# Residual added by accumulating DMAs, and no planned gap behind the output projection, in a fused attention and feed-forward kernel

## The chip, the cores and the metric

The kernel runs on one core of one Trainium2 chip. The metric is the device time of one execution in microseconds (us), as the median of several runs. The core has TensorE (PE in the profile; its weight loads are PEld), VectorE (DVE), ScalarE (ACT), GpSimd (POOL) and SyncE (SP). SyncE, ScalarE and GpSimd each issue DMAs from a queue of their own; here almost all are issued by SyncE and GpSimd.

## The reference

```python
# x: 1 x 2048 x 640, float32; 32 heads of 20; window of 8 keys, 2 positions apart
xn = layernorm(x)
q, k, v = split(xn @ wqkv)                      # 640 x 1920
logits = q . k[pos - 2 * (0..7)] * 20 ** -0.5   # masked where pos - 2w < 0
o = softmax(logits) . v[pos - 2 * (0..7)]
s = o @ wo                                      # 640 x 640
g = silu(silu(xn @ w1) @ w2)                    # 640 x 1536, 1536 x 640
return x + s * g
```

The last line is the one that matters: a product `s * g` and then the residual `x`.

## The kernel before

The 2048 rows are worked in four groups (0 to 3) of 512 rows, as tiles of 4 x 128 rows. Row tiles are chosen so that a position's window lies in its own partition and its neighbours. All matrix products run in three passes on operands split in a high and a low part (`hi x hi`, `lo x hi`, `hi x lo`), so each weight has two halves. A weight is split on chip at first use (ScalarE makes the high part, VectorE or GpSimd the low part, from a raw copy); its halves are stored to DRAM and loaded from there later (L584, on GpSimd's queue) into a ring of seven slots, `w`. Units of weights are loaded in the order in which TensorE uses them. w1 and w2 are split and stored in the first group; wo is split in the second and third group and loaded in the fourth.

For each group g there are two stages. In the projection stage TensorE makes q, k and v for four quarters of the heads (L1000 to L1002) while VectorE works on the attention: long multiplies and reductions over `pr` (L794, L797, L836, L842). In the feed-forward stage TensorE runs "ups" (w1, L1188 to L1190, into `rot`) and "downs" (w2, L1045 and L1047, into `acc`), with, between up 0 and up 1, the output projection of the group before, `wo_phase(g - 1)`, which also uses L1045 and L1047. After each up, ScalarE writes `sh` and `sf` (L1201, L1202) and VectorE the low part `sl = sf - sh` (L1203), which the last passes of the down read. So the output projection of group 0 lies in the feed-forward stage of group 1 (the second group) and that of group 1 in the stage of group 2 (the third). Those are the two that the change touches; groups 2 and 3 leave by other code (`wo_rest`, `wo_last`).

At the end of `wo_phase` VectorE multiplies the products in PSUM by the gate `G` (named `gate` in the profile), in place (L1084): four of 384 columns and two of 2 x 256. A planner entry named "hold" of HOLD = 3.4 us on VectorE follows; it emits no instruction. Then for each of the four row tiles SyncE loads x into one of three `xr` tiles (L1101), GpSimd adds the gated tile (L1102), and SyncE stores the sum to the output (L1104).

`G` has a second use: its 2560 columns, cut in five pieces of 512, are buffers for the transposes of the next group's normalized x by DMA (ScalarE rearranges, L677; SyncE transposes, L682; ScalarE joins, L690; L696 and VectorE's L697 split into `th` and `tl`). A piece can be taken once the tiles of `G` under it are no longer needed: piece 3 lies under tiles 2 and 3, piece 4 under tile 3. The `xr` tiles also receive raw copies of weights (L548).

The order of each engine's instructions is made ahead of time by a planner, `Weave`: every step is entered with its engine, an estimated duration, a priority, what it reads and writes, and extra times (`late` delays a reader on another engine, `more` is added to a DMA's landing). The planner simulates them in time and then changes the order where its simulated TensorE has a gap. An entry marked `lock` excludes other such entries on VectorE and GpSimd at the same time. The resulting order is fixed on each engine; on the chip an instruction waits, in that order, for what it reads and writes.

Of the kernel before, what the change touches and what calls it, by code (L numbers as in the profile page):

```python
# [15 lines left out]
P = 128  # L16
# [17 lines left out]
XQ = 1  # L34
ADD_LATE = 3
WARM, WARM2 = 20, 3
HOLD = 3.4
LO = 10
FIRST = """00 01 000 001 010 020 011 10 002 012 003 11 013 110 120 014 102 104 111 103 121 021 004 123 20 113 023 21 101 220 114
200 223 202 024 211 204 221 201 124 112 212 100 30 210 203 213 022 122 222 31 214 224 300 301 302 303 304 310 311 312  # L40
# [17 lines left out]
O_OUT = (), (35.0, 55.0), (35.0, 55.0), (10.0, 25.0, 40.0)  # L58
O_BACK = (), (80.0, 82.0), (80.0, 82.0), (40.0, 55.0, 60.0)
O_HOME = {2: {0: -9.0, 1: -6.0, 2: -3.0}}  # L60
BY_SCALAR = True
MULT = 400
WHOLE_O = (2,)
# [9 lines left out]
STORE_Q = 1, 3  # L73
STORE_W2 = ()
RAW_AGAIN = {}
AGAIN_AHEAD = 6
SHARED = (1, 0), (1, 2), (2, 0), (2, 2), (3, 0)
X_AT = 1.2, 6, 8
TILE_AT = 1, 1.5, 5, 6
# [254 lines left out]
def local_attention_silu_ffn(ctx: ExitStack, tc: tile.TileContext, x, wqkv, wo, w1, w2, out):  # L334
# [26 lines left out]
    def tiles(name, n, shape, dtype=F32):  # L361
        return [sb.tile(shape, dtype, name=f"{name}{i}") for i in range(n)]
# [27 lines left out]
    L = tiles("l", 2, [P, T, W, HQ])  # L390
    XIN = sb.tile([P, T, D], F32, name="xin")
    G = sb.tile([P, T, D], F32, name="gate")
    XR = tiles("xr", 3, [P, D])
    SF = sb.tile([P, TOK], F32, name="sf")
    MARK = small("mark", 1)
    TURN = sb.tile([P, TOK], F32, name="turn")
# [26 lines left out]
    def dve(n, fn, reads, writes, prio, lock=False, late=0.0, spans=()):  # L423
        return add("DVE", dv(n), fn, reads, writes, prio, lock, late=late, spans=spans)

    def act(n, fn, reads, writes, prio, table=None, more=0.0, late=0.0, at=0.0, spans=()):
        return add("ACT", ac(n) + more, fn, reads, writes, prio, table=table, late=late, at=at, spans=spans)
# [9 lines left out]
    def dma(fn, reads, writes, nbytes, prio, dur=0.45, more=0.0, quick=0.0, at=0.0):  # L437
        add("SP", dur, fn, reads, writes, prio, nbytes=nbytes, more=more, quick=quick, at=at)
# [71 lines left out]
    def raw_tile(k):  # L510


        if k < DC:
            return "pr", k
        if k < early:
            s = (k - DC) % 6
            return ("xr", s) if s < 2 else ("g", s - 2)
        return "xr", k % 3

    def raw_ap(u, r):  # L520
# [9 lines left out]
    def raw_load(k):  # L530
        i = fresh[k]
        u = units[i]
        n = width(i)
        of, s = raw_tile(k)
        raw_in[of, s] = k
        if of == "pr":
            r, kr = PRV[:, s * n:(s + 1) * n], [PRK[s]]
        elif of == "g":
            r, kr = G[:, s, :n], [("g", s, 0), ("g", s, CA)]
        else:  # L540
            r, kr = XR[s][:, :n], [("xr", s)]
        raws[i] = r, kr
        pairs = [raw_ap(u, r)]
        by = nc.scalar if k in BY_ACT else nc.sync

        def go():
            for to, frm in pairs:
                by.dma_start(to, frm)  # L548
        if k in BY_ACT:
            add("ACT", 0.65 * len(pairs), go, [], kr, -1, nbytes=n * P * 4)  # L550
            return
        dma(go, [], kr, n * P * 4, 1 + k if k < 2 * DC else clock[0] + 5, (0.62 if k < 2 * DC else 0.45) * len(pairs))

    def ahead(i):
        return AGAIN_AHEAD if units[i][0] == "w2" and i > fresh[early] else RAW_AHEAD
# [502 lines left out]
    def gate(ts, cs):  # L1058
        return of(G[:, ts.start] if ts.stop - ts.start == 1 else G[:, ts], cs)

    def gkeys(ts, cs):
        return [("g", t, cs.start) for t in range(ts.start, ts.stop)]
# [3 lines left out]
    def wo_phase(g, i):  # L1066
        banks = tm_banks()
        a, b = banks
        for c in range(DC):
            wh, wl, kh, kl = w_next("wo", c)  # L1070
            for t in range(T):
                def one(c=c, t=t, wh=wh, wl=wl):
                    tm_mm(banks, t, OH[i][:, c, tsl(t)], wh, c == 0, False)
                    tm_mm(banks, t, OH[i][:, c, tsl(t)], wl, False, False)
                    tm_mm(banks, t, OL[i][:, c, tsl(t)], wh, False, c == DC - 1)
                pe(3 * TM, one, t_keys(i, [c], [t]) + [kh, kl], [a[t][1], b[t // 2][1]])
            w_done()
        for p, kp, ts, cs in tm_views(banks):
            n = (ts.stop - ts.start) * (cs.stop - cs.start)
            if g == NG - 2 and BY_SCALAR:  # L1080
                at = of(XIN[:, ts.start] if ts.stop - ts.start == 1 else XIN[:, ts], cs)
                act(n, lambda p=p, at=at: nc.scalar.activation(at, p, AF.Copy), [kp], [("xin", t) for t in range(ts.start, ts.stop)], 0)
                continue
            dve(n, lambda p=p, ts=ts, cs=cs: nc.vector.tensor_tensor(  # L1084
                out=gate(ts, cs), in0=p, in1=gate(ts, cs), op=OP.mult), [kp], gkeys(ts, cs), 0, late=ADD_LATE)
        for t in range(T) if g == NG - 2 and BY_SCALAR else ():
            one = slice(t, t + 1)
            dve(D, lambda t=t: nc.vector.tensor_tensor(out=G[:, t], in0=XIN[:, t], in1=G[:, t], op=OP.mult),
                [("xin", t)], gkeys(one, slice(0, CA)) + gkeys(one, slice(CA, D)), MULT, lock=True)
        if g == NG - 2:  # L1090
            for t in range(T):
                xr, kx = (XR[t], [("xr", t)]) if t < 3 else (PRV[:, :D], PRK)
                rest.append((t, xr, kx))
                if t < 3:
                    dma(lambda t=t, xr=xr: nc.sync.dma_start(xr, rows(xg, g)[:, t, :]), [], kx, P * D * 4, clock[0] + 5, at=clock[0])
            return
        add("DVE", HOLD, lambda: None, [("g", t, CA) for t in range(T)], ["hold"], 0)
        for t in range(T):
            s = take("xr", 3)
            xr = XR[s]  # L1100
            dma(lambda t=t, xr=xr: nc.sync.dma_start(xr, rows(xg, g)[:, t, :]), [], [("xr", s)], P * D * 4, clock[0] + 5)  # L1101
            add("POOL", po(D), lambda t=t, xr=xr: nc.gpsimd.tensor_tensor(out=xr, in0=xr, in1=G[:, t, :], op=OP.add),  # L1102
                [("g", t, 0), ("g", t, CA)], [("xr", s)], 500, lock=True)
            dma(lambda t=t, xr=xr: nc.sync.dma_start(rows(og, g)[:, t, :], xr), [("xr", s)], [], P * D * 4, clock[0] + 20, quick=OUT_IN)  # L1104
# [124 lines left out]
    def ffn_phase(g, i, ix, io):  # L1229
        if g + 1 < NG:  # L1230
            behind = [("kv", XQ, 0)] if g else []
            step = 1 if g in X_SINGLE else 2
            for t in range(0, T, step):
                load_x(g + 1, t, step, behind=behind)
            for t in range(T):
                ln_stats(t)
            ln_rstd(0, T)
            for t in range(T):
                ln_apply(t)
        ps = None  # L1240
        begun = clock[0]
        by_dma = X_DMA.get(g, ())
        bufs = [("buf", c, h) for c in range(DC) for h in range(2)] if g else []
        if not g:
            for k, c in enumerate(by_dma):
                turn_first(c, ix, begun + X0_OUT + X0_PACE * k, begun + X0_BACK + X0_PACE * k)
        for kind, f in plan(g):
            if kind == "w1":
                up(g, i, f, io)
            elif kind == "wo":  # L1250
                wo_phase(g - 1, io)
                if g == NG - 1:
                    turn_os(g, io, begun)
                if g == NG - 1:
                    free_for([("xin", t) for t in range(T)], [("xin", t, c) for t in range(T) for c in (0, CA)])
                for c in range(DC) if by_dma else ():
                    ts = slice(c * TOK // D, ((c + 1) * TOK - 1) // D + 1)
                    free_for(gkeys(ts, slice(0, CA)) + gkeys(ts, slice(CA, D)), bufs[2 * c:2 * c + 2])
                for k, c in enumerate(by_dma):
                    by = (piece(G, X_BY[c]), ("buf", X_BY[c])) if c in X_BY else (TURN, ("turn",))  # L1260
                    turn_x(c, ix, by, (piece(G, c), ("buf", c)), clock[0] + PACE0[g] + PACE * k, clock[0] + BACK[g])
            elif kind == "x":
                if f not in by_dma:
                    split_t(XIN, [("xin", t) for t in range(T)], f, ix, (TH, TL), XIN[:, :, tsl(f)])
            elif kind == "o":
                if f not in O_DMA.get(g, ()):
                    o_chunk(g, f, io)
            elif kind == "rest":
                o_rest(g, f, io)
            else:  # L1270
                ps = ps or tm_banks()
                down(f, ps)
        for p, kp, ts, cs in tm_views(ps):
            n = (ts.stop - ts.start) * (cs.stop - cs.start)
            act(n, lambda p=p, ts=ts, cs=cs: nc.scalar.activation(gate(ts, cs), p, AF.Silu), [kp], gkeys(ts, cs) + bufs * bool(by_dma), 0, "silu")
        if g < NG - 1:
            turn_os(g, i, begun)
            turn_home(g, i)
# [40 lines left out]
```

## Time and profile before

| | |
|---|---|
| median of 3 runs | 597.69 us (597.64 to 597.71) |
| profiled execution, its own time | 598.14 us |
| its span, first to last instruction | 596.0 us |
| PE, PEld busy | 589.7 us (99%), 555.0 us (93%) |
| DVE, ACT, POOL busy | 514.1 (86%), 258.8 (43%), 163.2 us (27%) |
| granted TensorE clock | 1.000 |
| DMA | 165.00 MB, mean 277 GB/s |
| L1102, the residual adds on POOL | 8 of 1560 ns |

A row of a group of instructions gives line, engine, operation, output <- inputs, shape and count, then the busy time in us and the mean ns of one, then the engine's idle time just before them and what ended it. A timeline row gives the start, the duration, the engine, the line and what it writes and reads; "xN" at its end means that N instructions in a row are merged. Matmuls are pipelined, so their durations overlap; the distance between two starts is what one of them costs.

### The profile page before, as it was taken

The numbers are of one execution on the slowest core, as the hardware profiler recorded it, in microseconds if no ns is written. First come the engines' busy times: TensorE is split into PE (matmuls) and PEld (weight loads), VectorE is DVE, ScalarE is ACT, GpSimd is POOL, SyncE is SP. The second block draws the span as 40 slices with busy tenths as digits, with TensorE's granted clock in tenths as the row PEclk, the third lists the DMA queues.
The fourth block names the chain that finished last, engine by engine and source line by source line (L and its number), as shares of the span: only waits on it lengthen the run. The fifth ranks groups of instructions, "written<-read, shape, count | busy, mean of one in ns | idle before, by whom it ended". The sixth has DMA issues, their size and how long they took to land.

```text
span 596.0 us, 9084 instructions
## 1 busy us (share of the span) xinstructions
PE 589.7 (99%) x3431; PEld 555.0 (93%) x3431; DVE 514.1 (86%) x503; ACT 258.8 (43%) x458; POOL 163.2 (27%) x229
## 2 busy tenths in 40 slices
PE   8999999999999999999999999999999999999997
PEld 7999999999999999999999999989999999999997
DVE  6599999999799978999988997999847799999544
ACT  5447465362545323747523605433742254434230
POOL 5800102132210154342321126443122233531100
PEclk9999999999999999999999999999999999999999
DMA  9999999779999999997699999967779999989952
GB/s 287 317 307 333 322 411 394 287 254 292 278 321 315 318 216 231 375 223 217 196 308 310 303 348 308 301 196 232 197 214 291 286 289 261 263 221 316 253 195 89
DMA packets 83527, 165.00 MB, mean 277 GB/s; under 512 B 23213, under 2 KB 47501, under 8 KB 83485
## 3 DMA queue, kind: packets, MB, share of 16 engines
q1 hardware_dynamic: 63645, 84.72, 49.6%
q0 software_dynamic: 19296, 79.31, 45.3%
q8 instruction: 27, 0.44, 0.3%
q10 hardware_dynamic: 544, 0.41, 0.2%
q14 instruction: 15, 0.12, 0.1%
HBM read 107.91 MB, written 34.16 MB: 238 GB/s over the span
## 4 chain that ended last, share of the span: by engine, by line
PE 79%; issue 7%; DMA 7%; DVE 4%; POOL 2%; ACT 0%; SPq 0%; POOLq 0%; DVEq 0%
PE acc L1045 18%; PE acc L1047 12%; PE rot L1188 8%; PE rot L1190 8%; PE rot L1189 8%; PE acc L1000 7%; PE acc L1001 7%; PE acc L1002 7%; DMA half_wo<-w 3%; PE acc L950 2%; DMA w<-half_q 2%; DMA w<-half_w 1%; POOL w L584 1%; DVE pr L794 1%; DVE l L797 1%
## 5 line engine op out<-in xcount | busy, mean ns | idle before, releaser
L1000 PE MATMUL acc<-w,th 128*128 128x480 f32 x300 | 110.4, 368 | 0.0
L1001 PE MATMUL acc<-w,tl 128*128 128x480 f32 x300 | 109.8, 366 | 0.0
L1002 PE MATMUL acc<-w,th 128*128 128x480 f32 x300 | 109.8, 366 | 0.0
L1045 PE MATMUL acc<-w,sh 128*128 128x384 f32 x384 | 108.6, 328 | 0.0
L1047 PE MATMUL acc<-w,sh 128*128 128x256 f32 x384 | 104.7, 273 | 0.0
L794 DVE TENSOR_TENSOR pr<-q,kv 128x2560 f32<-128x2560 f32 x32 | 92.0, 2874 | 10.7 <-DMA kv<-kv 7.9
L836 DVE TENSOR_TENSOR pr<-q,kv 128x2560 f32<-128x2560 f32 x32 | 91.5, 2859 | 1.0
L1188 PE MATMUL rot<-th,w 128*128 128x512 f32 x240 | 91.8, 383 | 0.0
L1189 PE MATMUL rot<-tl,w 128*128 128x512 f32 x240 | 91.0, 379 | 0.0
L1190 PE MATMUL rot<-th,w 128*128 128x512 f32 x240 | 91.0, 379 | 0.0
L797 DVE TENSOR_REDUCE l<-pr 128x128 f32<-128x2560 f32 x32 | 89.7, 2804 | 0.3
L1201 ACT ACTIVATE sh<-rot 128x512 fp32r<-128x512 f32 x48 | 28.8, 599 | 122.2 <-PE rot L1190 122.2
L584 POOL DMA_DIRECT2D w<-half_w x72 | 38.9, 541 | 142.9 <-PE acc L1047 57.2
L1047 PEld LDWEIGHTS acc<-w,sh 128*128 128x128 f32 x384 | 73.7, 192 | 0.6
L1045 PEld LDWEIGHTS acc<-w,sh 128*128 128x128 f32 x384 | 72.6, 189 | 0.6
L1002 PEld LDWEIGHTS acc<-w,th 128*128 128x128 f32 x300 | 56.7, 189 | 4.0
L584 POOL DMA_DIRECT2D w<-half_q x52 | 27.9, 537 | 118.9 <-PE acc L1002 73.5
L1001 PEld LDWEIGHTS acc<-w,tl 128*128 128x128 f32 x300 | 56.7, 189 | 3.9
L1000 PEld LDWEIGHTS acc<-w,th 128*128 128x128 f32 x300 | 56.7, 189 | 3.9
L1045 PE MATMUL acc<-w,sl 128*128 128x384 f32 x192 | 56.0, 329 | 0.0
L1203 DVE TENSOR_TENSOR sl<-sf,sh 128x512 fp32r<-128x512 f32 x48 | 38.7, 807 | 19.0 <-ACT sf L1202 19.0
L1047 PE MATMUL acc<-w,sl 128*128 128x256 f32 x192 | 52.3, 273 | 0.0
(117 smaller groups left out, 1072.8 us busy)
## 6 DMA issues: line engine op xcount, KB each, us to landing
w<-half_w POOLq DMA_DIRECT2D x72, 640.0 KB, 6.8
w<-half_q POOLq DMA_DIRECT2D x52, 480.0 KB, 4.7
half_w<-w SPq DMA_DIRECT2D x24, 640.0 KB
half_q<-w SPq DMA_DIRECT2D x20, 480.0 KB
kv<-kv SPq DMA_DIRECT2D x15, 560.0 KB
w<-half_wo POOLq DMA_DIRECT2D x10, 640.0 KB, 8.3
kv<-kv SPq DMA_DIRECT2D x15, 420.0 KB
gate<-in_B_w_dram SPq DMA_DIRECT2D x16, 320.0 KB
```

The source lines that it names most:

```text
L584: add("POOL", 1.0, lambda: nc.gpsimd.dma_start(both, src), [("half", u)], [kh, kl], due + 10, nbytes=2 * n * P * 4)
L794: dve(2560, lambda: nc.vector.tensor_tensor(out=PR, in0=win(qq[:, t:t + 2, :], W, 0), in1=win(kv[:, 0, t:t + 2, :], W, CQ), op=OP.mult), h ...
L797: dve(2560, lambda: nc.vector.tensor_reduce(out=l[:, t:t + 2].rearrange("p t w h -> p (t w h)"), in_=PR.rearrange("p t w (h d) -> p (t w h ...
L836: dve(2560, lambda: nc.vector.tensor_tensor(out=PR.rearrange("p t w (h d) -> p t (w h) d", d=DH), in0=e[:, t:t + 2].rearrange("p t w h -> ...
L1000: nc.tensor.matmul(o, hi, vh, start=c == 0, stop=False)
L1001: nc.tensor.matmul(o, lo, vh, start=False, stop=False)
L1002: nc.tensor.matmul(o, hi, vl, start=False, stop=c == DC - 1)
L1045: nc.tensor.matmul(a[t][0][:, :CA].rearrange("p (m h) -> p m h", h=2), st, col_a(w), start=first, stop=last)
L1047: nc.tensor.matmul(b[t // 2][0][:, h * CB:(h + 1) * CB].rearrange("p (m h) -> p m h", h=2), st, col_b(w), start=first and h == 0, stop=las ...
L1188: nc.tensor.matmul(to, wh[:, cs], hi, start=c == 0, stop=False)
L1189: nc.tensor.matmul(to, wh[:, cs], lo, start=False, stop=False)
L1190: nc.tensor.matmul(to, wl[:, cs], hi, start=False, stop=c == DC - 1)
```

## The change

With ACCUM set, for groups 0 and 1, VectorE writes the gated products of row tiles 0 to 2 into `xr` and those of tile 3 back into `G[:, 3]`; the second wide product is split in two of 256 columns, since its halves go to different tiles. GpSimd then issues, for each row tile, a DMA that adds x from DRAM onto the tile in place, and SyncE stores the tile. The loads of x and GpSimd's adds are gone. The planner counts ACCUM_LATE = 3 us more for the landing of such a DMA. HOLD becomes 0.1. The three `xr` tiles become one tile with three parts. AGAIN_AHEAD becomes 9, and raw copies of w2 units that are split again after the first group would go to `spent` parts of the key and value buffer.

```diff
-HOLD = 3.4
+HOLD = 0.1
+ACCUM = True
+ACCUM_LATE = 3.0
-AGAIN_AHEAD = 6
+AGAIN_AHEAD = 9
+AGAIN_LATE = 0.0
-    XR = tiles("xr", 3, [P, D])
+    XRS = sb.tile([P, 3, D], F32, name="xr")
+    XR = [XRS[:, k, :] for k in range(3)]
...
+        if ahead(fresh[k]) == AGAIN_AHEAD:
+            return "spent", k % 4
...
+            if g < NG - 2 and ACCUM:
+                for v, us in ((p, ts),) if ts.stop < T or n < 512 else ((p[:, :1], slice(2, 3)), (p[:, 1:], slice(3, 4))):
+                    t, m = us.start, us.stop - us.start
+                    to = XRS[:, t:t + m] if t < 3 else G[:, 3:]
+                    to, v = (of(to, cs), v) if len(v.shape) == 4 else (of(to[:, 0], cs), v)
+                    ks = [(("gx", u, cs.start) if u < 3 else ("g", u, cs.start)) for u in range(t, t + m)]
+                    dve(n * m // (ts.stop - ts.start), lambda v=v, to=to, us=us, cs=cs: nc.vector.tensor_tensor(
+                        out=to, in0=v, in1=of(G[:, us], cs) if len(v.shape) == 4 else gate(us, cs), op=OP.mult),
+                        [kp] + [k for k in gkeys(us, cs)], ks + [("xr", u) for u in range(t, min(t + m, 3))], 0, late=ADD_LATE)
+                continue
...
-        for t in range(T):
+        for t in range(T) if ACCUM else ():
+            at, kg = (XR[t], [("xr", t)]) if t < 3 else (G[:, t], [("g", t, 0), ("g", t, CA)])
+            add("POOL", 1.0, lambda t=t, at=at: nc.gpsimd.dma_start(at, rows(xg, g)[:, t, :], accum_op=OP.add), [], kg, clock[0] + 5,
+                nbytes=P * D * 4, more=ACCUM_LATE)
+            dma(lambda t=t, at=at: nc.sync.dma_start(rows(og, g)[:, t, :], at), kg, [], P * D * 4, clock[0] + 20, quick=OUT_IN)
+        for t in range(T) if not ACCUM else ():
...
+        spent = [(k, 0, t) for k in ("kv", "own", "val") for t in range(T)] + [("partial", 0)] + halo_keys(0)
+        if g == NG - 2:
+            free_for(spent, [("spent", k) for k in range(4)])
...
+        if g == NG - 2:
+            free_for([("spent", k) for k in range(4)], spent)
```

More of the change, by code (lines that the diff above doesn't have):

```diff
@@ L539, in raw_load @@
             r, kr = G[:, s, :n], [("g", s, 0), ("g", s, CA)]
+        elif of == "spent":
+            r, kr = KV[0][:, s // 2].rearrange("p t m -> p (t m)")[:, s % 2 * D:(s % 2 + 1) * D], [("spent", s)]
         else:
@@ L551, in raw_load @@
             return
-        dma(go, [], kr, n * P * 4, 1 + k if k < 2 * DC else clock[0] + 5, (0.62 if k < 2 * DC else 0.45) * len(pairs))
+        dma(go, [], kr, n * P * 4, 1 + k if k < 2 * DC else clock[0] + 5, (0.62 if k < 2 * DC else 0.45) * len(pairs),
+            more=AGAIN_LATE if ahead(i) == AGAIN_AHEAD else 0.0)
     def ahead(i):
```

## The prediction

> **What bounds the kernel now.** I read the page's busy line first, then busy time by stretches, then the waits of TensorE, then the timeline at each place where TensorE lost time.
>
> ```profile
> span 596.0 us, 9084 instructions
> PE 589.7 (99%) x3431; PEld 555.0 (93%) x3431; DVE 514.1 (86%) x503; ACT 258.8 (43%) x458; POOL 163.2 (27%) x229
> ...
> 0.00:20.00 20.00, 17.64 (x94) 15.53 (x95) 12.12 (x42) 10.18 (x26) 11.82 (x17) 1.00 0.95 315
> 20.00:590.00 570.00, 569.96 (x3323) 537.60 (x3322) 500.05 (x458) 248.60 (x433) 151.39 (x213) 1.00 0.96 277
> 590.00:596.00 6.00, 2.08 (x18) 1.89 (x16) 1.97 (x4) 0.00 (x0) 0.00 (x0) 0.97 0.31 109
> ...
> PE rot L934 <- DVE xin L924: 1.0, 1, 1.0
> PEld acc L1045 <- DVE sl L1203: 0.3, 1, 0.3
> ```
>
> The three stretches (length, then the busy time of PE, PEld, DVE, ACT and POOL, the granted clock, the DMA share and GB/s) say it all: from 20 to 590 us TensorE is busy for 569.96 of 570.00 us at a clock of 1.00. What it lacks, 2.36 us before 20 and 3.92 us after 590, lies in the first group's opening and in the last group's exit, neither of which the change touches. Matmuls overlap, so "busy" can hide a short stall; the starts show those. The only wait of TensorE's loads on work in the middle is the 0.3 us on a subtraction (L1203), and this is it, with what led to it:
>
> ```profile
> 389.49 0.33 PE L1045 MATMUL acc<-w,sh 128*128 128x384 f32 x1
> 389.66 0.27 PE L1047 MATMUL acc<-w,sh 128*128 128x256 f32 x1
> 389.97 0.43 PE L1045 MATMUL acc<-w,sl 128*128 128x384 f32 x1
> 390.24 0.27 PE L1047 MATMUL acc<-w,sl 128*128 128x256 f32 x1
> 390.35 0.33 PE L1045 MATMUL acc<-w,sl 128*128 128x384 f32 x1
> ...
> 381.24 4.58 DVE L794 TENSOR_TENSOR pr<-q,kv 128x2560 f32<-128x2560 f32 x1
> 389.24 0.68 DVE L1203 TENSOR_TENSOR sl<-sf,sh 128x512 fp32r<-128x512 f32 x1
> ...
> 381.56 1.56 POOL L1102 TENSOR_TENSOR xr<-xr,gate 128x640 f32<-128x640 f32 x1
> ```
>
> An undisturbed pair steps by 0.17 us from L1045 to L1047 (389.49 to 389.66) and by 0.11 us from L1047 to L1045 (390.24 to 390.35). Here the steps are 0.31 (389.66 to 389.97) and 0.27 us (389.97 to 390.24): 0.20 + 0.10 = 0.30 us lost, because `sl` came at 389.24 + 0.68 = 389.92. VectorE was late since its multiply of 381.24 took 4.58 us with a GpSimd residual add (L1102) beside it.
>
> So the ceiling for any gain in these stages is 0.3 us, or 0.05%. The question is whether the change opens a new stall.
>
> **The change part by part.** The residual adds run in two stages, the feed-forward stages of the second and third groups.
>
> ```profile
> L1102 POOL TENSOR_TENSOR xr<-xr,gate 128x640 f32<-128x640 f32 x8 | 12.5, 1560 | 0.1
> L584 POOL DMA_DIRECT2D w<-half_w x72 | 38.9, 541 | 142.9 <-PE acc L1047 57.2
> L794 DVE TENSOR_TENSOR pr<-q,kv 128x2560 f32<-128x2560 f32 x32 | 92.0, 2874 | 10.7 <-DMA kv<-kv 7.9
> ...
> L1084 DVE TENSOR_TENSOR gate<-acc,gate 128x384 f32<-128x384 f32 x8 | 4.0, 546 | 0.0
> L1084 DVE TENSOR_TENSOR gate<-acc,gate 128x512 f32<-128x512 f32 x4 | 2.7, 678 | 0.0
> L1139 DVE TENSOR_TENSOR gate<-acc,gate 128x256 f32<-128x256 f32 x3 | 1.2, 415 | 0.0
> ...
> 213.92 1.85 DVE L1203 TENSOR_TENSOR sl<-sf,sh 128x512 fp32r<-128x512 f32 x1 [2.43 <-ACT sf L1202]
> 213.66 1.56 POOL L1102 TENSOR_TENSOR xr<-xr,gate 128x640 f32<-128x640 f32 x1
> ```
>
> *GpSimd's adds go.* Eight adds of 1.56 us, 12.5 us of an engine that is busy for 27%. Their price lay on VectorE: the subtraction at 213.92 takes 1.85 us instead of 0.68, ending when the add that began at 213.66 is over plus about its own time; the multiply at 381.24 takes 4.58 instead of its mean 2.87. The first excess is 1.2 us, the second 1.7; eight adds at 0 to 1.7 us free 0 to 14 us of VectorE, and I take 8 x 1.2 = 9 us. None of it is on TensorE's path except the last one: minus 0.30 us, from nothing (the new order puts another late subtraction there) to 0.30. I take 0.30.
>
> *Accumulating DMAs come.* Eight issues on GpSimd's queue; no row shows the accumulating kind. The nearest is an issue of 640 KB of weights, 0.54 us; eight at half to three times that are 2 to 13 us of GpSimd, against the 12.5 us that go. I take 4.3 us. Off the path by itself; what it can delay are the weight loads behind it (below).
>
> *SyncE loses its eight loads of x* into `xr` (320 KB each), the same bytes now come on GpSimd's queue. The eight stores stay, and now wait for a DMA's landing instead of an add.
>
> *The products.* VectorE writes them to `xr` (tiles 0 to 2) or in place (tile 3), and splits one 512-wide product into two of 256: 2 x 0.415 - 0.678 = 0.15 us more for each stage, 0.3 us of VectorE in all, off the path. Their inputs and places in TensorE's order are the same. Reading `xr` out of the weights' raw copies is over before: TensorE has used those weights by then.
>
> *HOLD from 3.4 to 0.1.* No instruction goes; the planner may put VectorE's next operation 3.3 us earlier in its plan. What can go before an urgent subtraction is a long attention multiply of 2.87 us.
>
> *Ring space for the x transposes.* Pieces 3 and 4 of `gate` were free once the add had read tile 3; now they are free once tile 3's store has read it. In the second group's stage these rows hold:
>
> ```profile
> 223.12 0.53 SPq L1104 DMA_DIRECT2D out_dram<-xr  x1
> 223.70 18.53 SPq L548 DMA_DIRECT2D xr<-in_A_wo_dram  x2
> 251.32 2.64 SPq L682 DMA_TRANSPOSE gate<-turn  x2
> 254.01 1.28 SPq L682 DMA_TRANSPOSE gate<-gate  x1
> ...
> 208.35 3.14 DVE L1084 TENSOR_TENSOR gate<-acc,gate 128x384 f32<-128x384 f32 x6
> 283.70 0.68 DVE L697 TENSOR_TENSOR tl<-xin,th 128x512 fp32r<-128x512 f32 x1
> ```
>
> A raw load that waits for the store of 223.12 holds SyncE until 223.70 + 18.53 = 242.2, so a store lands within some 19 us here, and the transposes into `gate` pieces come at 254 anyway. With the accumulate issued behind the products (208.35 + 3.14 = 211.5), landed within the 13.0 us of the slowest weight load (row below) and stored within 19 us, tile 3 is free at about 243.5: estimate, 10 us before the transpose wants it. If that cover were gone, the join at 283.70 would slip by as much, and the next projection with it.
>
> *The rest of the diff does nothing here.* The look-ahead of 9 and the "spent" buffers apply to w2 units that are split again after the first group; w2 is kept in its halves at first use and loaded afterwards, so there are none. The two added planner entries have zero length and emit nothing.
>
> **The cover of the weight loads** decides most of it:
>
> ```profile
> DMA to landing us min/median/max: 4.6/8.9/13.0
> ...
> 222.89 0.53 POOL L584 DMA_DIRECT2D w<-half_w  x1 [2.72 <-PE acc L1047]
> 242.00 0.33 PE L1045 MATMUL acc<-w,sh 128*128 128x384 f32 x1
> ...
> DMA to landing us min/median/max: 4.2/6.6/10.1
> ...
> 357.63 0.57 POOL L584 DMA_DIRECT2D w<-half_w  x1 [5.71 <-PE rot L1190]
> 370.84 0.38 PE L1188 MATMUL rot<-th,w 128*128 128x512 f32 x1
> ...
> 208.00:226.00 18.00, 18.00 (x116) 17.17 (x115) 14.11 (x12) 3.23 (x5) 9.94 (x11) 1.00 1.03 217
> ```
>
> The first landing line is for L584 from 205 to 250 us, the second from 340 to 395. Loads go in the order of use, seven ring slots ahead: the load issued at 222.89 is the w2 strip that TensorE starts at 242.00, 19.1 us later; the one of 357.63 is the w1 strip of 370.84, 13.2 us later. With the slowest landing of each window, at least 19.1 - 13.0 = 6.1 and 13.2 - 10.1 = 3.1 us of slack stay. Four accumulates bring 4 x 320 KB = 1.31 MB; at the 217 GB/s of this stretch that is 6.0 us of transfer, at double bytes (the destination is read too) 12.1, at none (it replaces loads of the same size) 0. Delay 0 to 12 us; I take 3, half of 6.0, because half the traffic is not new and the accumulates start at about 211, before the slowest loads, when the waiting loads are used later than 230. 3 us is under both slacks.
>
> **The sum** against the profiled execution's 598.14 us (span 596.0): VectorE - 9 + 0.3, GpSimd - 12.5 + 4.3, both 0 on the path; TensorE - 0.30; new stalls 0: 597.84. The median of the runs shown is 597.69, 0.45 below; there it makes 597.4.
>
> **The rivals.** *A, slower: weights wait behind accumulates in GpSimd's queue.* Place: the strips of 242 and 371 us. TensorE stalls once a load is more than 6.1 (or 3.1) us later than its slowest now; beyond 4.3 to 7.3 us the 0.2% (1.2 us) is passed. At the bound of 12.1 us the stall is 6.0 to 9.0: 603.4 to 606.4; at 6.0 us of delay it is 0 to 2.9: up to 600.3. For it: the DMA share is 1.03 there, the transposes crowd the same time, and GpSimd's queue runs in order, so an accumulate that waits for VectorE's product holds the loads behind it. Against: that wait is for products that ran by 211.5, and 1.31 MB of loads go. The Trainium skill, DMA: Bandwidth & Descriptors, section Two DMAs through the same engine are not ordered, has descriptors of one queue start in order, which is what would put the weights behind the accumulates. Its section Anatomy of one DMA — SWDGE (gpsimd) path gives 2.0 us plus bytes/436e3 for a DMA from GpSimd; by it four accumulates of 327,680 bytes one after the other would take an estimated 11.0 us and give 602.3 to 605.3; if most of the 2.0 is completion, as the page also says, they take 3.0 us and nothing stalls. No run yet shows which.
>
> *B, slower: VectorE's order.* Without the gap a long multiply stands before a subtraction that TensorE needs:
>
> ```profile
> 363.67 3.12 DVE L1203 TENSOR_TENSOR sl<-sf,sh 128x512 fp32r<-128x512 f32 x1 [3.83 <-ACT sf L1202]
> 366.02 0.33 PE L1045 MATMUL acc<-w,sl 128*128 128x384 f32 x1
> ```
>
> The subtraction of 363.67 (the first of two in that row) feeds the matmul of 366.02: with 0.68 us of its own, 1.7 us of room, against 2.87 us of a multiply. One such collision costs 1.2 us, two 2.4: 598.6 to 599.8. Against: that subtraction was late because ScalarE stood behind two GpSimd adds, which go; VectorE idles 3.83 us just there.
>
> *C, faster by over 0.2%.* It would take 1.2 us of idle TensorE; the middle has 0.3. Only the opening (2.36) or the exit (3.92) could give it, and nothing there changes: 596.4 or less.
>
> **How the numbers follow.** 0.2%, 1.2 us, is about what a measurement of this kernel can tell from no change. Forecast 0.77: 597.4, within 597.1 to 598.8 (a few small stalls of 0.3 in a new order). A 0.10 (599 to 606), B 0.11, C 0.02. A single collision of B that costs 1.2 us ends at 598.6, inside the 0.2%; I give that 0.02 of the 0.11: slower 0.19, same 0.79, faster 0.02. The range takes in B with two collisions and the lower cases of A; above 599.8 some 0.08 is left, below 597.1 some 0.03.
>
> **What would show it.** Right: no L1102; no 4.6 us multiply beside GpSimd; VectorE at about 505 us; TensorE still 569.9 of 570 from 20 to 590; no wait on L1203 at 390. A: TensorE waits for L584 or its landing lines rise past 19 us, in 225 to 250 or 365 to 390. B: TensorE waits for L1203 with a multiply just ahead of it. The prediction fails if the accumulating kind costs much more than its bytes, or if the new order collides in later stages, which I can't see from here.

## The result, and the profile after

The changed kernel is slower: 615.61 us (median of 4 runs, 613.51 to 616.33) against 597.70 (4 runs, 597.64 to 597.71); ratio 1.0285, 95% interval 1.0255 to 1.0315. The profiled execution took 613.51 us. The prediction was 597.4, with a range up to 599.8: wrong, by 18 us. Below, the ratio leaves out runs more than 1.5% above their kernel's fastest, so where the runs of one kernel differ by 20 us the median and the count of all its runs stand beside it.

The page of after: the busy line, and the 40 slices of TensorE and of its granted clock.

```profile
span 611.6 us, 9085 instructions
PE 594.4 (97%) x3431; PEld 558.2 (91%) x3431; DVE 507.9 (83%) x505; ACT 256.6 (42%) x458; POOL 161.3 (26%) x229
...
PE   8999999999999999976899999999999999999997
...
PEclk9999999999999999997899999999999999999999
```

Before had a 9 in every slice from the second on but the last. After has lost three slices of 15 us, the 18th to the 20th, 260 to 306 us, and a part of the clock with them. By stretches, before and then after (columns as in the prediction):

```profile
200.00:320.00 120.00, 120.00 (x699) 113.21 (x698) 106.94 (x95) 48.31 (x75) 41.80 (x60) 1.00 1.02 263
```

```profile
20.00:590.00 570.00, 558.52 (x3210) 524.82 (x3210) 487.96 (x447) 244.37 (x429) 149.07 (x213) 0.99 1.02 275
200.00:320.00 120.00, 108.52 (x619) 101.17 (x618) 94.34 (x81) 43.66 (x65) 37.82 (x53) 0.96 1.09 218
320.00:588.00 268.00, 268.00 (x1575) 252.89 (x1574) 226.69 (x194) 108.79 (x187) 75.10 (x118) 1.00 1.02 272
```

All of TensorE's lost time between 20 and 590 lies in 200 to 320: 120.00 - 108.52 = 11.5 of 570.00 - 558.52 = 11.5 us. From 320 to 588, where the third group's stage is, it is busy throughout. The DMA engines are no less busy in the bad stretch (1.09 against 1.02) but move less: 218 against 263 GB/s. They work longer for each byte. Steps between starts of TensorE's matmuls, summed over 200 to 320 against their medians, give 16.1 us lost: four gaps of 7.4, 1.9, 1.8 and 1.1 us (12.1) and 3.9 in some 24 steps at about twice their length, in two stretches, from 278.4 to 282.4 and from 295.8 to 299.5.

The largest gap, and the doubled steps after it:

```profile
270.86 0.38 PE L1214 MATMUL rot<-th,w 128*128 128x512 f32 x1
278.44 0.79 PE L1212 MATMUL rot<-th,w 128*128 128x512 f32 x1 [7.20 <-ACT sf L1226]
279.02 0.63 PE L1213 MATMUL rot<-tl,w 128*128 128x512 f32 x1
...
282.40 0.38 PE L1212 MATMUL rot<-th,w 128*128 128x512 f32 x1
```

From 279.02 a step is 0.43 us instead of 0.22, until 282.40 (8 steps in 3.4 us): after 7.2 us of idling TensorE works for some 4 us (278.44 to 282.40) at half the clock, 0.50 in the trace. The Trainium skill, TensorE: Matmul & The Clock Gate, section What's actually happening, has the clock at half after an idle window of about 3.4 us and back after about 3.4 us of work; this trace agrees, with 4.0 us. The second stretch agrees less: the gaps ahead of it, from 286.9 to 295.8, are of 1.9, 1.8 and 1.1 us, each shorter than such a window, and the clock is 0.50 all the same.

Who was late: waits of after in this stage (engine, what waited, for what: us in total, times, longest), and ScalarE's timeline.

```profile
ACT xin L699 <- DMA gate<-turn: 15.3, 1, 15.3
...
ACT kv L699 <- DMA kv<-kv: 8.7, 1, 8.7
...
PE rot L1212 <- ACT sf L1226: 7.2, 1, 7.2
...
PE acc L1054 <- ACT sh L1225: 3.4, 2, 1.8
```

```profile
273.04 1.34 ACT L699 ACTIVATE xin<-gate 128x1024 uint16<-128x1024 uint16 x1 [15.29 <-DMA gate<-turn]
...
277.30 0.60 ACT L1225 ACTIVATE sh<-rot 128x512 fp32r<-128x512 f32 x1
277.79 0.59 ACT L1226 ACTIVATE sf<-rot 128x512 f32<-128x512 f32 x1
```

ScalarE's join of a transposed piece of x (L699, which was L690) idles 15.29 us for its DMA transpose. Behind it in ScalarE's order stand `sh` and `sf` of an up; they come at 277.30 and 277.79, TensorE goes on at 278.44. In before none of these waits is there between 225 and 300 us. So the transposes are late. SyncE's queue shows how in its timeline, and in the group of its issues (ns min/median/max), each of after; the last fence is the group of before:

```profile
239.76 6.19 SPq L556 DMA_DIRECT2D xr<-in_A_wo_dram  x3
246.04 4.50 SPq L691 DMA_TRANSPOSE gate<-turn  x2
250.59 7.60 SPq L691 DMA_TRANSPOSE gate<-gate  x1
258.29 13.63 SPq L691 DMA_TRANSPOSE kv<-kv  x2
```

```profile
L691 SPq DMA_TRANSPOSE gate<-gate x4: 3159/5787/7599, 250.6 to 281.0; - x4
L691 SPq DMA_TRANSPOSE kv<-kv x4: 1513/2108/12038, 258.3 to 288.5; - x4
```

```profile
L682 SPq DMA_TRANSPOSE gate<-gate x4: 1277/1517/1710, 254.0 to 261.9; - x4
L682 SPq DMA_TRANSPOSE kv<-kv x4: 1189/1384/1652, 255.4 to 271.6; - x4
```

They do not begin late: at 246.04, where before began at 251.32. They are slow. One issue takes up to 12.0 us, before at most 1.7, and the join at 273.04 comes 27.0 us after the first of the two transposes that it reads was issued. And the weight loads issued between 250 and 300 landed in (after, then before):

```profile
DMA to landing us min/median/max: 5.0/20.0/23.7
```

```profile
DMA to landing us min/median/max: 3.4/4.1/7.7
```

The accumulating DMAs themselves, as a group and in GpSimd's timeline:

```profile
L1119 POOL DMA_DIRECT2D xr<-in_A_x_dram x6: 917/1288/1641, 210.1 to 376.7; - x6
L1119 POOL DMA_DIRECT2D gate<-in_A_x_dram x2: 1935/1966/1996, 211.8 to 377.2; - x2
...
DMA to landing us min/median/max: 8.5/11.5/15.7
```

```profile
210.09 2.73 POOL L1119 DMA_DIRECT2D xr<-in_A_x_dram  x3
211.78 1.94 POOL L1119 DMA_DIRECT2D gate<-in_A_x_dram  x1
212.79 1.49 POOL L593 DMA_DIRECT2D w<-half_w  x1
```

Two tables from the records of the single DMA packets and semaphores describe "slow". The first has the mean time of a packet in ns (and the count), by size and time of start. The second has when the 16 parts of one weight load landed, by its time of issue: first / 8th / last. The Trainium skill, DMA: Bandwidth & Descriptors, section Why a DMA increments its semaphore by 16 and not by 1, has each of the 16 engines add one when its own share has landed; the 16 increments are read that way here.

```
                          210 to 224 us            246 to 289 us
                     2560 B       5120 B        256 B (transposes)  5120 B (weights)
before               110 (256)    401 (386)      36 (5120)          252 (902)
after, accumulating  279 (501)    317 (208)     112 (3481)          355 (943)

weight load          before                       after
issued near 223-225  231.41/233.11/235.87         231.17/234.45/238.74
near 249             252.34/252.51/253.59         256.88/266.80/267.09
near 262             269.60/269.67/269.75         274.63/274.95/285.87
```

An accumulating packet takes 279 ns where a plain one of SyncE took 110. A transpose's packets of 256 bytes, 36 ns before, take 112. In before the 16 engines are 4.5 us apart near 223 and 1.3 near 249, when the transposes begin at 251; in the loads during these they are within 0.5. In after they are 5.7 to 7.7 us apart in the loads issued from 224 to 234, which land before the transposes begin, and 10 to 11 us in the loads of 249 and 262, while the transposes run.

### The profile page after: what moved, and what is told of

Its sections match the earlier page's. It is cut to its first block, busy times and chain, and to the rows that moved or that the text cites. A ratio compares the mean times of both kernels' runs of the same rounds, so it can differ in the third digit from the quotient of the medians.

```text
span 611.6 us, 9085 instructions
## 1 busy us (share of the span) xinstructions
PE 594.4 (97%) x3431; PEld 558.2 (91%) x3431; DVE 507.9 (83%) x505; ACT 256.6 (42%) x458; POOL 161.3 (26%) x229
## 4 chain that ended last, share of the span: by engine, by line
PE 92%; DMA 3%; SPq 2%; ACT 1%; DVE 1%; issue 1%
PE acc L1054 20%; PE acc L1056 13%; PE acc L1009 10%; PE acc L1010 10%; PE acc L1011 10%; PE rot L1212 8%; PE rot L1213 8%; PE rot L1214 8%; DMA gate<-gate 3%; SPq L691 2%; PE acc L959 2%; PE rot L655 1%; DMA xin<-in_A_x_dram 1%; PE rot L943 0%; PE rot L1195 0%
## 5 line engine op out<-in xcount | busy, mean ns | idle before, releaser
L593 POOL DMA_DIRECT2D w<-half_w x72 | 41.3, 598 | 142.3 <-PE acc L1056 54.8
L1212 PEld LDWEIGHTS rot<-th,w 128*128 128x128 f32 x240 | 45.9, 191 | 13.5 <-ACT sf L1226 7.6
```

The costliest lines, as they stand in the source:

```text
L593: add("POOL", 1.0, lambda: nc.gpsimd.dma_start(both, src), [("half", u)], [kh, kl], due + 10, nbytes=2 * n * P * 4)
L1212: nc.tensor.matmul(to, wh[:, cs], hi, start=c == 0, stop=False)
```

## The experiments

The theory after this reading, D: accumulating DMAs ahead of the x transposes in the second group's stage leave the 16 DMA engines out of step; transposes and weights beside each other then crawl; ScalarE's ordered wait hands this to TensorE. The rivals: HOLD (VectorE's order); the bytes or the waits of the new chain, not the kind; the third group's stage; joins that merely stand too early in ScalarE's order. Each run is compared with the kernel before on the same chip.

### The same order with plain loads

```diff
-nc.gpsimd.dma_start(at, rows(xg, g)[:, t, :], accum_op=OP.add)
+nc.gpsimd.dma_start(at, rows(xg, g)[:, t, :])
```

> The changed kernel with the eight accumulating DMAs issued as plain loads into the same places, so the groups 0 and 1 leave x alone in the output and the product s * g is left out there. Every engine's order is the same, instruction for instruction. Theory K (the accumulating kind: packets of 2560 bytes took about 230 ns each in the trace against 108 for plain ones, and after them the DMA engines run out of step, so that the transposes of x that follow crawl and ScalarE waits 15.3 us for one): within 3 us of before, 597 to 600, and no wait of ScalarE on a transpose over 3 us in 255 to 275. Theory O (the new order alone, which puts transposes and joins 5 us earlier, onto raw loads and weights): 611 to 616, with the same wait. If the traffic on GpSimd's queue, of either kind, matters rather than the kind: in between or as O, with the engines' landings apart as in the changed kernel.

Measured: median 597.52 of 10 runs (8 within 596.98 to 597.95, then 601.51 and 615.67); before 597.98 (31 runs, 596.98 to 601.01); ratio 0.9989 (0.9968 to 1.0010). Every engine's instructions stand in the changed kernel's order, HOLD included. Issue and landing of the eight DMAs, and SyncE's queue:

```profile
L1119 POOL DMA_DIRECT2D xr<-in_A_x_dram x6: 536/548/561, 209.8 to 359.1; - x6
...
DMA to landing us min/median/max: 5.3/6.7/8.4
```

```profile
237.66 2.51 SPq L691 DMA_TRANSPOSE gate<-turn  x2
240.53 1.19 SPq L691 DMA_TRANSPOSE gate<-gate  x1
242.43 2.63 SPq L691 DMA_TRANSPOSE kv<-kv  x2
245.10 3.95 SPq L691 DMA_TRANSPOSE gate<-gate  x3
263.02 2.53 SPq L691 DMA_TRANSPOSE kv<-kv  x2
```

So it is the kind, and not the order, that makes the loss of 18 us the rule: the order, the bytes on GpSimd's queue and the waits of the stores cost nothing in nine of ten runs. The kind brings its packet size with it: as plain loads the eight DMAs run in 512 packets of 5120 bytes, accumulating in 1024 of 2560, and no run parts the two. The engines are within 0.4 us of each other in the weight loads from 224 to 249, and the mean 256-byte packet takes 24 ns (5120 packets, 236 to 268 us). But one run in ten was at 615.67: a loss of this size also happens without accumulating, though no trace shows what it was in that run.

### HOLD alone

```diff
 # the kernel before
-HOLD = 3.4
+HOLD = 0.1
```

> The kernel before with HOLD = 0.1 alone; loads of x and GpSimd's adds stay. Theory H (the missing gap makes the bad order): 608 or more, with ScalarE waiting for a transpose near 260. Theory K: 597 to 599; at most small waits on the subtraction L1203.

Measured: 597.54 (10 runs, 596.84 to 602.51); ratio 1.0008 (0.9981 to 1.0036). VectorE's order is not the cause.

### The accumulating DMAs with HOLD at 3.4

```diff
 # the kernel after
-HOLD = 0.1
+HOLD = 3.4
```

> The changed kernel with HOLD back at 3.4, so accumulating DMAs alone. Theory K: slow again, 606 to 618, with the wait of ScalarE on a transpose in the second group's stage. Theory H: 597 to 599.

Measured: median 602.72 of 10 runs, five of 596.89 to 598.94 and five of 606.51 to 619.68. The ratio is 0.9985 (0.9963 to 1.0007). The 606 to 618 that was expected came in half of the runs only. The kind makes the loss likely; the order around it, which HOLD shifts, seems to decide how likely (5 of 10 here, 8 of 8 in the changed order). The five near 597 show that it need not cost anything. The profiled run, 598.94, shows how: its transposes crawl too (single issues of up to 7.2 us, three of `gate` in 17.43 us from 251.44), ScalarE waits 5.2 us for one, and weight loads issued from 250 to 300 take up to 15.5 us; but the x transposes begin at 240.20, 6 us before those of after, and TensorE loses 1.4 us of 200 to 320. A crawl and a loss are thus two things; by these traces the loss comes where the transposes end too late for the joins.

### Accumulating in the third group's stage only

```diff
-ACCUM = True
+ACCUM = (1,)
-            if g < NG - 2 and ACCUM:
+            if g in ACCUM:
...
-        for t in range(T) if ACCUM else ():
+        for t in range(T) if g in ACCUM else ():
...
-        for t in range(T) if not ACCUM else ():
+        for t in range(T) if g not in ACCUM else ():
```

> The changed kernel with accumulating DMAs in the third group's stage only; in the second group's stage x is loaded and GpSimd adds as before, HOLD is 0.1. All of the loss in the trace (TensorE stalls at 271, 287, 292 us and the half clock after them) lay in the second group's stage. Theory K with its place: 597 to 599. If the third group's stage has a loss of its own once the second has none: 600 or more. Theory H: 608 or more.

Measured: 597.86 (10 runs, 597.35 to 602.43); ratio 1.0006 (0.9984 to 1.0027). The profiled run, 600.41, idles 1.9 us at 376.5 for a weight load and 0.9 at 512, and nothing from 200 to 320. The place of the loss is the second group's stage. The 1.9 us are a stall of the kind that the prediction's rival A foresaw for the third group's stage: TensorE waits for a weight load issued behind accumulating DMAs.

### The changed kernel again

No edit.

> The changed kernel again, beside the others of this call on one chip, since the spread between runs turned out to matter (HOLD back at 3.4 with accumulating DMAs gave 596.9 to 619.7). Theory D (the accumulating kind sets the 16 DMA engines apart by 1 to 3 us over four DMAs, and transposes that meet engines apart crawl, by chance more or less): mostly above 606, some runs possibly near 597; in a slow profile the last of the 16 landings of a weight load comes 3 us or more behind the eighth between 215 and 260. Theory O (this order is bad by itself): all at 611 to 617.

Measured: 611.90 (4 runs, 610.15 to 614.74) against 597.49 (15 runs, 596.91 to 606.64); ratio 1.0238 (1.0195 to 1.0280). The x transposes crawl again, and the longest wait is at another join:

```profile
ACT kv L699 <- DMA kv<-kv: 14.5, 1, 14.5
...
PE acc L1054 <- ACT sh L1225: 6.1, 1, 6.1
```

### No DMA transposes of x in the second group's stage

```diff
-X_DMA = {1: (0, 1, 2, 3, 4), 2: (2, 3, 4)}
+X_DMA = {1: (), 2: (2, 3, 4)}
```

> The changed kernel with the second group's stage transposing the next x on TensorE instead of by DMA (five chunks, 4 transposes each: 5 x 0.44 us, and 0.08 us behind each, 2.6 us more of TensorE). Theory D: the crawl has nothing to crawl there, 599.5 to 601 with a narrow spread, whatever the accumulating DMAs do to the engines. If weights late behind the accumulating DMAs are the cause (rival A of the prediction): still 605 or more, with TensorE waiting for L593.

Measured: 600.73 (6 runs, 599.61 to 602.19), ratio 1.0047 (1.0023 to 1.0071): the loss and its scatter are gone with these transposes, though the accumulating DMAs stay. Its profile, by stretch, weight loads from 250 to 300, and the four transposes that are left (attention outputs):

```profile
200.00:320.00 120.00, 120.00 (x707) 113.31 (x706) 103.18 (x86) 39.84 (x69) 40.77 (x58) 1.00 0.89 252
```

```profile
DMA to landing us min/median/max: 3.5/4.0/6.8
```

```profile
L691 SPq DMA_TRANSPOSE kv<-kv x4: 1191/1275/1339, 237.6 to 266.1; - x4
```

TensorE loses nothing there, the weight loads land as in before, and the four transposes are fast. The 3 us are 20 transposes on TensorE (3451 matmuls instead of 3431) at 0.11 us a step, 2.2 us, and in the profiled run a stall of 1.6 at 378.66, again for a weight load of the third group's stage. The engines were apart here too after the accumulating DMAs (load of 224.42: 230.53 to 231.75) and had closed to 0.05 us by the load of 235.63; they stayed within 0.9 until 264. So in this run the spread closes by itself, with four transposes beside it instead of ten.

### Plain loads with twice the bytes

```diff
+            def load(t=t, at=at):
+                nc.gpsimd.dma_start(at, rows(xg, g)[:, t, :])
+                nc.gpsimd.dma_start(dram.tile([P, D], F32, name=f"more_{g}_{t}"), rows(xg, g)[:, t, :])
-            add("POOL", 1.0, lambda t=t, at=at: nc.gpsimd.dma_start(at, rows(xg, g)[:, t, :], accum_op=OP.add), [], kg, clock[0] + 5,
+            add("POOL", 1.0, load, [], kg, clock[0] + 5,
```

> The plain loads of e1 with a second DMA of the same 320 KB behind each, from x to a scratch place in DRAM: more bytes on GpSimd's queue than the accumulating kind reads and writes, none of them accumulating. x is left out of groups 0 and 1 as in e1. Theory D (the kind sets the engines apart): 597 to 600 in most runs, engines within 0.5 us between 212 and 225. Rival Q (the queue's backlog, some 6 to 8 us of weights late, is what the transposes meet): 605 or more in most runs.

Measured: median 597.88 of 10 runs; seven of 596.88 to 598.41, three of 609.30 to 613.87; ratio 0.9995 (0.9980 to 1.0010). The profiled run was one of the three, at 611.59, with the same picture and no accumulating DMA anywhere:

```profile
L691 SPq DMA_TRANSPOSE gate<-gate x4: 1983/3881/11948, 252.4 to 272.3; - x4
L691 SPq DMA_TRANSPOSE kv<-kv x4: 1522/3144/4959, 254.7 to 282.9; - x4
```

The kind is thus one way into the crawl and not the only one. Double bytes gave 3 in 10, against 1 in 10 with single ones; ten runs of each can't tell these apart.

### Joins planned later

```diff
+    slow = [SLOW]
...
-                [ka + (h,)], [kb + (h,)], P * TOK * 6, at + 2, ISSUE, SLOW)
+                [ka + (h,)], [kb + (h,)], P * TOK * 6, at + 2, ISSUE, slow[0])
...
+                    slow[0] = 22 if g == 1 and k >= 2 else SLOW
                     turn_x(c, ix, by, (piece(G, c), ("buf", c)), clock[0] + PACE0[g] + PACE * k, clock[0] + BACK[g])
+                    slow[0] = SLOW
```

> The changed kernel, with the planner told that the transposes of chunks 2 to 4 in the second group's stage take 22 us more to land instead of 8, so that ScalarE's joins stand later in its order. Theory D with ScalarE's in-order queue as what hands the delay to TensorE: TensorE's stall near 271 goes, 600 to 608; what is left is x that comes late for the projection. If the transposes being late for the projection is all that counts: 611 to 617 still.

Measured: 612.16 (4 runs, 602.95 to 615.63), ratio 1.0147 (1.0065 to 1.0230). Theory D's 600 to 608 was missed: later joins are no cure, so their place in ScalarE's order isn't all that counts. In the profiled run, 613.72, TensorE now waits 4.0 us for weights, and 6.8 us for ScalarE (L1306), whose joins (L701) had waited 14.7 us for transposes.

```profile
ACT kv L701 <- DMA kv<-kv: 14.7, 2, 8.1
...
PE acc L1011 <- ACT gate L1306: 6.8, 1, 6.8
...
PE rot L1214 <- DMA w<-half_w: 4.0, 1, 4.0
```

### How many accumulating DMAs it takes

Three kernels with the changed kernel's order on every engine, in which only some of the eight DMAs accumulate:

```diff
-nc.gpsimd.dma_start(at, rows(xg, g)[:, t, :], accum_op=OP.add)
+nc.gpsimd.dma_start(at, rows(xg, g)[:, t, :], **({"accum_op": OP.add} if g == 0 else {}))             # four, second group's stage
+nc.gpsimd.dma_start(at, rows(xg, g)[:, t, :], **({"accum_op": OP.add} if t < 2 else {}))              # two in each stage
+nc.gpsimd.dma_start(at, rows(xg, g)[:, t, :], **({"accum_op": OP.add} if (g, t) == (0, 0) else {}))   # one
```

> The order of every engine is that of the changed kernel, instruction by instruction. Only the kind differs: the four DMAs of x in the second group's feed-forward stage accumulate, the four in the third's are plain loads into the same places (so for the second residual group of output rows the kernel leaves x out, or the product). Theory D (accumulating DMAs ahead of the x transposes of the second group's stage put the DMA engines out of step, and the transposes, or the weights beside them, then come late): like the changed kernel, nearly all runs between 606 and 620 us, median 610 to 616, idle TensorE between 265 and 297 us. Rival E (the third group's accumulates are needed too): 597 to 600. Rival F (the kind sets only the odds, each accumulate adding to them): somewhere between, runs of 597 and of 610 mixed, more of the slow ones.

> The same order again. In both stages only row tiles 0 and 1 are brought by accumulating DMAs, tiles 2 and 3 by plain loads into the same places (x, or the product, is left out for those rows). If the kind sets the odds by its amount (rival F), half the accumulates give a mixture: 2 to 6 of 10 runs above 605 us, the rest near 597.5. If one accumulate in front of the transposes is enough (Theory D in its strict form), nearly all runs lie at 606 to 620. If the last accumulate, tile 3 in the gate's own columns, on whose store the transposes wait, is what counts (rival G), all runs lie near 597.5, as with plain loads.

> The changed kernel's order again, every engine's. One single DMA accumulates: row tile 0 in the second group's stage; the other seven are plain loads into the same places (x, or the product, is left out for those rows). Known so far with this order: no accumulate, 1 of 10 runs above 605 us; two in each stage, 6 of 6; four in the second group's stage, 5 of 6 (the sixth 604). If one accumulating DMA is enough to put the DMA engines out of step ahead of the transposes (Theory D, strict), most runs lie between 604 and 618 us. If the odds go with the number (rival F), runs of both kinds: 2 to 6 of 10 above 604. If a single one is absorbed (its packets fill a gap in the queue), as with plain loads: at most 1 of 10, median 597.5.

Measured, in one table with the same order's other runs:

```
accumulating DMAs            median us   all runs           above 604 us   ratio (95%)
none                         597.52      596.98 to 615.67    1 of 10       0.9989 (0.9968 to 1.0010)
one (second stage)           608.94      597.22 to 619.89   10 of 12       1.0034 (0.9990 to 1.0079)
two in each stage            610.52      605.99 to 615.81    6 of 6        1.0191 (1.0146 to 1.0236)
four in the second stage     612.59      604.33 to 620.94    6 of 6        1.0164 (1.0107 to 1.0221)
four in each (the change)    see above   610.15 to 616.33    8 of 8        1.0285, 1.0238
the kernel before            597.5-598.0 596.91 to 606.64    1 of 78
```

Four in the second group's stage do what the change does, so the third group's aren't needed. Two in front of the last, tile 3's, are enough as well, so it isn't the store of tile 3 that counts. One is nearly enough; of the theories on record the strict form of D comes closest, since 10 of 12 is more than the 2 to 6 of 10 of a proportional one. For "one" the counts say this, and not the ratio, which has three of the twelve runs in it. (In two profiled runs of these, TensorE lost time later too: with four at 423, 6.8 us with the clock, behind a weight load; with one at 578, 7.8 us, whose cause is open.) SyncE's queue of this kernel, in its profiled run of 619.89 us:

```profile
241.45 6.64 SPq L691 DMA_TRANSPOSE gate<-gate  x1
248.19 8.84 SPq L691 DMA_TRANSPOSE kv<-kv  x2
257.07 18.84 SPq L691 DMA_TRANSPOSE gate<-gate  x3
276.02 6.76 SPq L691 DMA_TRANSPOSE kv<-kv  x2
```

This row by row is the plain kernel's list: the gate transposes begin 1 us later (241.45 against 240.53), and three of them then take 18.84 us instead of 3.95. Neither a late store nor a late buffer is left as a cause. All its accumulates and plain loads of x landed in at most 8.3 us, where the plain kernel needed 8.4. Its weight load of 235.21, in flight when the transposes begin, has its engines 6.1 us apart (242.31 to 248.38), the plain kernel's of 235.32 0.1 us; the one before, of 233.26, 2.4 (239.47 to 241.84), the plain kernel's 0.1.

What stays open: why transposes crawl when the engines are apart. A spread is there before the x transposes run, and it grows while they run and closes without them; but no run set the spread by itself, and before goes through 4.5 us at 223 and 1.3 at 249 unharmed. With accumulating in the third group's stage only, the engines came 11.1 us apart with plain DMAs ahead of them (load of 252.52: 259.42 to 270.55), TensorE lost nothing in that stage, and two transposes issued at 276.77 took 2.50 us, as in before, while a load landed whose engines were still 5.6 us apart (274.50 to 280.06). A spread is therefore not enough by itself. As the link it is argued at most, while the two ends are shown: the kind ahead of them, and the transposes. No kernel here is faster than before beyond what can be told.

## Why the prediction was wrong, point by point

**What bounds the kernel: right.** TensorE bounds it, the ceiling of a gain was 0.3 us, and that stall did go: after and the plain kernel have no lost step at 390, and the plain kernel is what was forecast, 597.52 against 597.4.

**GpSimd's adds: right.** VectorE is busy 507.9 us (forecast about 505; it is 6.2 us less than before, and 8.7 were forecast), and no long multiply takes 4.6 us:

```profile
L803 DVE TENSOR_TENSOR pr<-q,kv x32: 2811/2823/2827, 33.7 to 543.6; 128x2560 f32<-128x2560 f32 x32
```

**The accumulating issues: size off, harmless.** 0.92 to 2.0 us each, but overlapping: the four of a stage hold GpSimd from 210.09 to the next load at 212.79, 2.7 us, and those of the other stage from 375.59 to 377.78, 2.2 us: 4.9 instead of 4.3, inside the bounds of 2 to 13.

**Ring space for the x transposes: the step that failed.** Its stated half held: tile 3 was free in time, and the transposes began 5 us before those of before. What it took without saying so was that a transpose, once issued, lasts as long as in before. It priced when the transposes may start and nothing else; an issue then took up to 12.0 us where before's slowest took 1.7. "If that cover were gone, the join ... would slip by as much, and the next projection with it" names the right chain (join, ScalarE, TensorE), but the join slipped with the cover in place.

**The cover of the weight loads: mis-sized, and looked for in the wrong window.** From 205 to 250 us the slowest landing rose from 13.0 to 18.4:

```profile
DMA to landing us min/median/max: 5.6/13.1/18.4
```

That is 5.4 us instead of 3, under the slack of 6.1: no stall at 242, as forecast. From 340 to 395 it rose from 10.1 to 16.8, 6.7 us and more than the slack of 3.1; after has no stall there, but two other profiled runs do (below). Bytes were the measure there (0, 6.0 or 12.1 us); the records have 512 accumulating packets of 279 ns over 16 engines, 8.9 us of their time. The 16 us more of 250 to 300 (23.7 against 7.7), long after the last accumulate landed at 227, had no term at all.

**Rival A: right engine, wrong mechanism for this loss.** It had weights waiting behind accumulates in order, at the strips of 242 and 371. The loss begins at 270.86, 29 us after the first. At the second the rival is seen in small: TensorE stalls for a weight load by 1.9 us at 376.5 with the third group's stage alone accumulating, and by 1.6 us at 378.66 without the x transposes. By the fit of the Trainium skill (DMA: Bandwidth & Descriptors, section Anatomy of one DMA — SWDGE (gpsimd) path) four in a row would take an estimated 11.0 us; here each lands 8.5 to 15.7 us after its issue, the last at 211.8 + 15.7 = 227.5. A rule of the same page of the Trainium skill, section Issuing engines are not separate DMA queues, is that DMAs of all issuers run on the same 16 engines and interleave. This case agrees: behind GpSimd's accumulating DMAs SyncE's transposes took up to 12.0 us. The rule gives no price, and none was in the trace of before.

**Rival B: wrong** (HOLD alone: 1.0008). Its room of 1.7 us was also misread: the row of 363.67 is one subtraction of 3.12 us and not the first of two, since there are 48 in before as in after, and it ended at 366.79, after the matmul of 366.02 had begun. **The half clock** after a gap, 3.9 of the 16.1 us, was in no rival's price.

**"The prediction fails if the accumulating kind costs much more than its bytes":** it does, though not where that was looked for. A chance of 0.19 for slower, ending at 606, was too small for a kind of operation that no row showed, beside a DMA share of 1.03.

## What to carry to other kernels

When a change brings a DMA of a kind that the trace hasn't got, ask what its packets do to the other traffic of the same 16 engines over the next 50 us, not only when it lands; transposes beside weight loads were the fragile part here. A step that starts 10 us early has cover for its start only; its duration needs one of its own. And before undoing a design, send the same order with the plain kind: that one run parted the kind from everything else in the diff.

## What was not expected of the hardware

- An accumulating DMA's 2560-byte packets took 279 ns on average beside 110 ns for plain ones of SyncE; its issue on GpSimd took 0.9 to 2.0 us, overlapping, instead of 0.55.
- One accumulating DMA of 320 KB moved 10 of 12 runs by 7.6 to 22 us, although in the profiled one it and its seven plain fellows landed within 8.3 us (all plain: 8.4). The time was lost 50 us and more after it.
- DMA transposes can crawl: 256-byte packets of 112 ns instead of 36 in the mean, an issue on SyncE of up to 12 us instead of 1.7, and 23.7 us for weight loads beside them that took at most 7.7. With plain loads one trace shows it too (611.59), and times like it came in 1 and 3 of 10 runs. It need not cost: one run of 598.94 has it.
- The 16 DMA engines can be 10 us apart in one and the same load, with plain DMAs ahead of it too (11.1 us in one trace), and where the x transposes were left out, 1.2 us closed to 0.05 within 11 us.
